# Second layer in the order of the code with follow-ups one block late, expert tokens fetched earlier, and a third float64 piece converted beside the experts

## The chip, the cores and the metric

The kernel runs on one core of a Trainium2 chip. The metric is the device time of one execution in microseconds. It was measured in three runs, and their median counts. A fourth execution was profiled, and its trace is what the rows below come from. Engines are named as in the profile: PE is the matrix engine and PEld its weight load, DVE the vector engine, ACT the scalar engine, POOL the GpSimd engine, and SP issues most transfers.

## What is computed

Attention on 2 x 8 heads of 576 tokens gives 1152 tokens of 512 numbers. A top-1 mixture of eight experts follows, then a second layer for all tokens, the part that most of the change concerns:

```python
h = np.maximum(np.einsum('ecd,edf->ecf', disp, w1), 0.0)   # 8 experts, 512 -> 1024
y = np.einsum('ecf,efd->ecd', h, w2)                        # 1024 -> 512
out[i] = gate_w[i] * y[expert_idx[i], pos[i]]               # kept tokens, others 0
...
h = x @ w_in                                                # 512 -> 2048
g = h * (1.0 / (1.0 + np.exp(-h)))
return (g @ w_out).astype(np.float32)                       # 2048 -> 512
```

The weights `w_in` and `w_out` arrive as float64. The kernel turns them into float32 with integer operations on their words.

## The kernel before

**Experts.** The sixteen units of `WSEQ` alternate: unit 0 is `w1` of expert 0, then `w1` of expert e and `w2` of expert e-1 in turn, so unit 5 is `w1` of expert 3. A `w1` unit multiplies the 192 tokens of its expert, which a transposing transfer (`load_x`, L712) puts into one of two tiles `xw`. Its weights are split into a high and a low float16 part: ACT squares them (L145), a matmul with ones sums over partitions (L150), ACT and DVE write the high halves (L189, L191), DVE the low halves (L196). A `w2` unit works in float32 (L782). Its result goes from `psy` to `yg` (`post_y`, L791, DVE), and ACT squares it (L798). `post_y` needs the gates: `gl` is written to memory and read back into `yg` (L698, L899). Between two units stands `rest()`, a test whether an expert has more than 192 tokens (L918). It has loops inside that don't run here.

**Conversion.** Eight pieces (`in` 0 to 3 and `out` 0 to 3) of 2 MB are each loaded (`c_load`, L843), converted in four parts of three DVE operations (`c_conv`, L850 to L852), squared on ACT (`c_sq`, L858), scaled (`c_scale`) and split, high on POOL (L881) and low on DVE (L882). These steps stand in a list `extra`, of which `task` and `more` take one after the other. Two staging tiles hold a piece: `stg` and `stg2`, the second in a tile of the experts' weights.

**Second layer.** `l1(j, n, fo)` is a block of 12 matmuls of 384 columns into one of four `psh` tiles. Behind it come a sigmoid on ACT (L1113), a product on DVE (L1115), a float16 copy on ACT (L1116) and a remainder on POOL (L1117). `l2(h, i, tt)` is a block of 24 matmuls of 256 columns into one of three `psy` tiles, with a copy on ACT (h = 0, L1135) or a sum on DVE (h = 1, L1137), and at the end a transfer of 128 rows to the output. Order: 24 blocks of `l1`, 18 of `l2`, 24, 18. `split_y` makes the two float16 parts of `yg` that `l1` reads: high (L1071 on ACT, L1073 on POOL) and low (L1074 on DVE).

**Order.** Each engine works through its own queue in order. Under `tc.manual_schedule` that queue is in the order of the code. Elsewhere the compiler's scheduler sets it. Before, units 0 to 3 and from unit 4 to `split_y` are in code order; the blocks of the second layer are the scheduler's.

Of the kernel before, what the change touches and what calls it, by code (L numbers as in the profile page):

```python
# [21 lines left out]
E = 8  # L22
# [14 lines left out]
def moe_kernel(tc, qL, qtL, kL, vL, sL, wgL, w1L, w2L, capL, winL, woutL, out):  # L37
# [680 lines left out]
    def moe_phases():  # L718
# [104 lines left out]
        seq = [("in", 0), ("in", 1), ("out", 0), ("out", 1), ("in", 2), ("in", 3), ("out", 2), ("out", 3)]  # L823
# [37 lines left out]
        def c_scale(m, j):  # L861
            ps = psy.tile([P, 512], F32, tag="y", name="psy")
# [8 lines left out]
        def c_split(m, j, q):  # L871
# [5 lines left out]
            else:  # L877
# [3 lines left out]
            G.tensor_scalar(hi, src, d["s"][q], 0.0, op0=ALU.mult, op1=ALU.add)  # L881
            V.scalar_tensor_tensor(out=lo, in0=src, scalar=d["s"][q], in1=hi,  # L882
                                   op0=ALU.mult, op1=ALU.subtract)
            if q == 3:
                d["done"] = True

        def c_tasks(m, j):
            t = [[] for _ in range(5)]
# [3 lines left out]
            t.append([lambda: c_scale(m, j)])  # L892
            for q in range(4):
                t.append([lambda q=q: c_split(m, j, q)])
# [89 lines left out]
        def unit0():  # L984
            load_x(1)
            slots0()
# [15 lines left out]
        def unit(u):  # L1002
# [5 lines left out]
            if kind == "w1":  # L1008
# [3 lines left out]
                if e < E - 1:  # L1012
                    load_x(e + 1)
# [3 lines left out]
            for q in range(4):  # L1017
# [26 lines left out]
        extra += [[lambda: c_load("in", 0)], []] + c_tasks("in", 0)  # L1044
        extra += [[lambda: c_load("in", 1)], []] + c_tasks("in", 1)
        extra[-1] += [lambda: c_load("out", 0), lambda: c_load("out", 1)]
        for u in range(4, NW):
            unit(u)
        flush(0)
        task(len(extra))  # L1050
        return xctx, cd, c_load, c_tasks, seq, ys, wint, psh, psy, yp, inv
# [3 lines left out]
    def moe2(xctx, cd, c_load, c_tasks, seq, ys, wint, psh, psy, yp, inv):  # L1055
# [5 lines left out]
        yh = y2p.tile([P, 2, 4, NTOK], F16, tag="yh", name="yh")  # L1061
        V.tensor_reduce(out=yt, in_=ysq, axis=AX.X, op=ALU.add)
        ps = pools["psn"].tile([P, 512], F32, tag="n", name="psn")
# [3 lines left out]
        def split_y(n):  # L1067
            a = slice(n * CH, (n + 1) * CH)
            for k in range(4):
                if n == 0:  # L1070
                    A.activation(out=yh[:, 0, k, a], in_=ys[:, k, a], func=AF.Copy, scale=sy)  # L1071
                else:
                    G.tensor_scalar(yh[:, 0, k, a], ys[:, k, a], sy, 0.0, op0=ALU.mult, op1=ALU.add)  # L1073
                V.scalar_tensor_tensor(out=yh[:, 1, k, a], in0=ys[:, k, a], scalar=sy, in1=yh[:, 0, k, a],  # L1074
                                       op0=ALU.mult, op1=ALU.subtract)

        split_y(0)
        k3, k4, rg = inv[:, 0:4], inv[:, 8:12], inv[:, 24:26]
        extra = []
# [3 lines left out]
        for i in range(2, 8):  # L1083
            extra += c_tasks(*seq[i])
            if i + 2 < 8:
                extra[-1].append(lambda i=i: c_load(*seq[i + 2]))
# [12 lines left out]

        def l1(j, n, fo):  # L1100
# [11 lines left out]
            sg = g2p.tile([P, CH], F32, tag="sg", name="sg")  # L1112
            A.activation(out=sg, in_=ps[:, 0:CH], func=AF.Sigmoid, scale=k3[:, j:j + 1])  # L1113
            r = g2p.tile([P, CH], F32, tag="r2", name="r2")
            V.scalar_tensor_tensor(out=r, in0=ps[:, 0:CH], scalar=C1, in1=sg, op0=ALU.mult, op1=ALU.mult)  # L1115
            A.copy(gt[n][:, 0, f, :], r)  # L1116
            G.tensor_tensor(out=gt[n][:, 1, f, :], in0=r, in1=gt[n][:, 0, f, :], op=ALU.subtract)  # L1117

        def l2(h, i, tt):
# [10 lines left out]
            if tt == 0:  # L1130
                if i == 0:
                    V.tensor_scalar(rg[:, h:h + 1], ry, inv[:, 16 + h:17 + h], 1.0 / C1, op0=ALU.mult, op1=ALU.mult)
                V.tensor_tensor(out=kc, in0=rg[:, h:h + 1], in1=cd["out", 2 * h + i]["r"], op=ALU.mult)
            if h == 0:
                A.activation(out=ot[:, tt, d], in_=o, func=AF.Copy, scale=kc)  # L1135
            else:
                V.scalar_tensor_tensor(out=ot[:, tt, d], in0=o, scalar=kc, in1=ot[:, tt, d],  # L1137
                                       op0=ALU.mult, op1=ALU.add)
            if h == 1 and i == 1:
                G.indirect_dma_start(out=out, out_offset=bass.IndirectOffsetOnAxis(ap=idl[:, tt:tt + 1], axis=0),  # L1140
                                     in_=ot[:, tt, :], in_offset=None)

        split_y(1)
        split_y(2)
        man2.close()
        ot = yp.tile([P, NT, DM], F32, tag="yg", name="ot")
# [278 lines left out]
```

## Time and profile before

| | us |
|---|---|
| median of 3 runs | 528.86 |
| lowest and highest | 525.57, 533.93 |
| profiled execution, its own time | 533.83 |
| its span, first to last instruction | 532.2 |

The profiled execution is 4.97 us slower than the median, and 1.63 us of its time lie outside the span. PE is busy in 86% of the span (459.8 us), but it is not busy evenly, so the views of single stretches say more than this share. Times in the rows are us from the start of the span.

### The profile page before, as it was taken

The page shows a single profiled execution, that of the slowest core. Times are in us where ns is not written, and L with a number is a line of the kernel's source. Part 1 is how long each engine was busy: PE and PEld are TensorE (multiplying, and loading weights), DVE is VectorE, ACT ScalarE, POOL GpSimd, SP SyncE. Part 2 cuts the span into 40 slices and gives each one's busy share as a digit, 9 for nine tenths or more (in the row PEclk, how much of TensorE's full clock was granted, in tenths as well). Part 3 has the DMA queues.
Part 4 walks back from the last instruction along what each step waited for, and adds up shares of the span by engine and source line. Part 5 has one row for each costly group of instructions (what it writes and reads, how often), then busy time and mean ns, then how long its engine had stood idle before and what let it go on. Part 6 is the DMA issues. An engine that isn't in the chain of part 4 may idle for free.

```text
span 532.2 us, 9871 instructions
## 1 busy us (share of the span) xinstructions
PE 459.8 (86%) x3788; PEld 375.4 (71%) x3789; DVE 321.7 (60%) x823; ACT 224.9 (42%) x443; POOL 206.3 (39%) x238
## 2 busy tenths in 40 slices
PE   0868579697899994999999987598999999999995
PEld 0744445386689993999999983364688876668885
DVE  8888669996665232954754369999337836321111
ACT  1666537585164305743642026355621534551000
POOL 9775577655136100003000207484541237542121
PEclk9977879999899997899999997899999999999999
DMA  8799999999938849996962171422004400000111
GB/s 153 236 180 219 194 216 217 254 239 201 257 120 276 240 162 292 405 352 205 309 212 91 69 275 43 156 60 101 2 2 160 159 1 0 1 1 20 60 52 49
DMA packets 97122, 83.05 MB, mean 156 GB/s; under 512 B 70112, under 2 KB 74400, under 8 KB 96816
## 3 DMA queue, kind: packets, MB, share of 16 engines
q1 hardware_dynamic: 94112, 76.02, 53.7%
q0 software_dynamic: 1728, 4.76, 2.7%
q10 hardware_dynamic: 1232, 1.61, 1.2%
q8 instruction: 31, 0.51, 0.4%
q14 instruction: 19, 0.16, 0.1%
HBM read 58.07 MB, written 7.91 MB: 124 GB/s over the span
## 4 chain that ended last, share of the span: by engine, by line
PE 42%; DVE 10%; DMA 10%; issue 3%; POOL 1%; ACT 1%; SPq 0%; POOLq 0%; DVEq 0%; ACTq 0%
PE psy L1127 13%; PE psh L1108 11%; PE psy L782 10%; PE psh L753 8%; DMA stg<-in_moe_w_out_dram 3%; DMA xw<-table 2%; DVE cx L851 2%; DMA gl<-gk 2%; DVE yh L1074 2%; DVE cx L850 1%; DVE stg L852 1%; DVE r L1115 1%; DMA meta<-table,srow 1%; DMA wst<-in_moe_w_dram 1%; DVE wout L882 1%
## 5 line engine op out<-in xcount | busy, mean ns | idle before, releaser
L1108 PE MATMUL psh<-yh,win 128*128 128x384 f16 x576 | 99.4, 335 | 9.8 <-DVE r L1115 8.0
L1127 PE MATMUL psy<-wout,g 128*128 128x256 f16 x864 | 95.6, 273 | 1.2 <-ACT ot L1135 1.2
L1108 PEld LDWEIGHTS <-win 128*128 128x128 f16 x576 | 57.6, 100 | 50.0 <-issue 9.5
L1127 PEld LDWEIGHTS <-g 128*128 128x128 f16 x864 | 84.6, 98 | 11.5 <-issue 1.4
L340 PE MATMUL pss<-kt,qa 65*128 65x128 f32 (+3 forms) x128 | 52.8, 560 | 21.7 <-DVE wsp L303 12.0
L1117 POOL TENSOR_TENSOR g<-r,g 128x384 f16<-128x384 f32 x48 | 49.0, 1026 | 49.5 <-ACT g L1116 37.0
L881 POOL TENSOR_SCALAR win<-stg,sci 128x512 f16<-128x512 f32 x16 | 16.0, 1015 | 134.3 <-DVE sci L102 134.3
L753 PE MATMUL psh<-xw,wsp 128*128 128x192 f16 x672 | 60.2, 252 | 8.8 <-DMA xw<-table 8.8
L753 PEld LDWEIGHTS <-wsp 128*128 128x128 f16 x672 | 58.0, 101 | 10.1 <-issue 8.1
L1115 DVE SCALAR_TENSOR_TENSOR r<-psh,sg 128x384 f32<-128x384 f32 x48 | 26.5, 553 | 39.8 <-ACT sg L1113 39.7
L340 PEld LDWEIGHTS pss<-kt,qa 128*128 128x128 f32 (+1 forms) x128 | 26.8, 257 | 31.8 <-DVE nm L363 16.5
L381 ACT ACTIVATE et<-et,nm 128x128 f32<-128x128 f32 (+3 forms) x64 | 32.8, 554 | 28.1 <-DVE nm L363 28.1
L782 PE MATMUL psy<-h,wsp 128*128 128x192 f32 x256 | 42.6, 327 | 0.4 <-PEq L918 0.4
L405 POOL TENSOR_TENSOR hl<-et,hl 128x512 f16<-128x512 f32 (+3 forms) x34 | 35.9, 1066 | 16.9 <-ACT hl L400 15.1
L782 PE MATMUL psy<-h,wst 128*128 128x192 f32 x256 | 42.4, 327 | 0.0
L782 PEld LDWEIGHTS psy<-h,wsp 128*128 128x128 f32 x256 | 41.5, 190 | 0.7 <-PEq L918 0.7
L782 PEld LDWEIGHTS psy<-h,wst 128*128 128x128 f32 x256 | 41.5, 190 | 0.0
L758 ACT ACTIVATE h<-psh 128x384 f32<-128x384 f32 x32 | 15.6, 487 | 57.4 <-PE psh L753 53.3
L1116 ACT CAST g<-r 128x384 f16<-128x384 f32 x48 | 24.4, 508 | 28.1 <-DVE r L1115 28.1
L363 DVE CUSTOM_DVE_ANT_0 et<-pss,mk 128x128 f32<-128x128 f32 (+3 forms) x64 | 28.9, 479 | 9.8 <-POOL hl L405 9.5
L196 DVE SCALAR_TENSOR_TENSOR wsp<-wst,sci,wsp 128x2048 f16<-128x2048 f32 x12 | 28.1, 2339 | 9.1 <-ACT wsp L189 8.3
L1137 DVE SCALAR_TENSOR_TENSOR ot<-psy,inv,ot 128x256 f32<-128x256 f32 x18 | 8.7, 484 | 37.6 <-PE psy L1127 37.6
(248 smaller groups left out, 809.6 us busy)
## 6 DMA issues: line engine op xcount, KB each, us to landing
wst<-in_moe_w_dram SPq DMA_DIRECT2D x42, 512.0 KB, 6.0
wsp<-in_moe_w_dram SPq DMA_DIRECT2D x20, 512.0 KB, 7.7
stg<-in_moe_w_in_dram SPq DMA_DIRECT2D x16, 512.0 KB, 5.4
stg<-in_moe_w_out_dram SPq DMA_DIRECT2D x16, 512.0 KB, 5.5
table<-xh SPq DMA_DIRECT2D x4, 774.0 KB, 6.8
wst<-in_v_dram SPq DMA_DIRECT2D x2, 1024.0 KB, 5.7
kt<-in_k_dram SPq DMA_DIRECT2D x3, 512.0 KB, 7.9
qa<-in_q_dram SPq DMA_DIRECT2D x3, 512.0 KB, 6.1
```

Of the source, the lines that this page charges most:

```text
L196: V.scalar_tensor_tensor(out=d["sp"][:, 1, lo:hi], in0=d["st"][:, lo:hi], scalar=d["s"], in1=d["sp"][:, 0, lo:hi], op0=ALU.mult, op1=ALU.s ...
L340: PE.matmul(out=pv[:, j, :], lhsT=qa[c % 2][r, h, b, :], rhs=kt[r, h, b, 0:n], start=True, stop=True)
L363: maxi[i] = V.tensor_tensor_reduce(out=ev[:, j, :], in0=st[i]["s"][:, j, :], in1=mk[:, 512 - n:512], scale=-0.125, scalar=3.0e38, op0=ALU. ...
L381: A.activation(out=e[:, j, :], in_=e[:, j, :], func=AF.Exp, scale=-1.0, bias=st[i]["m"][j])
L405: spl[i] = (V if LO[i] == "V" else G).tensor_tensor(out=hl[:, w:w + n], in0=e, in1=hl[:, 0:n], op=ALU.subtract)
L753: PE.matmul(out=pv[:, j, :], lhsT=sp[:, cw, k, a], rhs=xw[e][:, 4 * cx + k, :], start=(n == 0 and k == 0), stop=(n == 2 and k == 3))
L782: PE.matmul(out=pv[:, j - js[0], :], lhsT=w[:, k, a], rhs=hh[e][:, k, :], start=(k == 0), stop=(k == 7))
L1108: PE.matmul(out=ps[:, 0:CH], lhsT=wv[:, cw, k, fo * P:(fo + 1) * P], rhs=yh[:, cy, k, a], start=(i == 0 and k == 0), stop=(i == 2 and k == 3))
L1115: V.scalar_tensor_tensor(out=r, in0=ps[:, 0:CH], scalar=C1, in1=sg, op0=ALU.mult, op1=ALU.mult)
L1116: A.copy(gt[n][:, 0, f, :], r)
L1117: G.tensor_tensor(out=gt[n][:, 1, f, :], in0=r, in1=gt[n][:, 0, f, :], op=ALU.subtract)
L1127: PE.matmul(out=o, lhsT=gt[n][:, cg, k, a], rhs=woutt[h][:, cw, k, d], start=(m == 0 and k == 0), stop=(m == 2 and k == 7))
```

## The change

It has four parts. The tokens of experts 1 and 2 are both fetched in unit 0, and those of expert e + 3 at the start of the `w2` unit of expert e; `rest()` moves from behind unit 3 to behind unit 4. The steps of a conversion are spread over twelve places of the list in place of ten, `in` 2 goes through the experts' stage in place of a part of `out` 0, and later pieces follow in another order. The second layer is put under `manual_schedule`, and what follows a block is issued behind the matmuls of the next block (`after1`) or of the next but one (`after2`). The parts of `yg` are made by ACT and DVE without POOL, the first 384 tokens ahead and the others two steps behind each of the first eight blocks.

```diff
@@ load order, conversion
-                if seq.index((m, j)) % 2 and len(cd) > 1:
+                if (m, j) in (("out", 0), ("in", 3), ("out", 3)):
...
-            ps = psy.tile([P, 512], F32, tag="y", name="psy")
+            ps = pools["psn"].tile([P, 512], F32, tag="n", name="psn")
...
+            t = [[] for _ in range(12)]
             for q in range(4):
                 t[q].append(lambda q=q: c_conv(m, j, q))
                 t[q + 1].append(lambda q=q: c_sq(m, j, q))
+                t[6 + q].append(lambda q=q: c_split(m, j, q, 0))
+                t[7 + q].append(lambda q=q: c_split(m, j, q, 1))
+            t[6].insert(0, lambda: c_scale(m, j))
+            if nxt:
+                t[11].append(lambda: c_load(*nxt))
@@ experts
         def unit0():
             load_x(1)
+            load_x(2)
...
-                if e < E - 1:
-                    load_x(e + 1)
+            elif k + 2 < E:
+                load_x(k + 2)
...
-                if u >= 4 and (q == 3 or q and kind == "w2"):
+                if u >= 5 and (q in (0, 3) or kind == "w2"):
...
-        for u in range(1, 4):
+        for u in range(1, 5):
...
+        c_load("in", 0)
+        extra += [[], []] + c_tasks("in", 0, ("in", 1)) + [[]] + c_tasks("in", 1, ("in", 2)) + [[]]
+        extra += c_tasks("in", 2, ("out", 1))
+        for u in range(5, NW):
+            if u == 13:
+                c_load("out", 0)
             unit(u)
         flush(0)
-        task(len(extra))
@@ second layer
+        extra += c_tasks("out", 0, ("in", 3)) + c_tasks("out", 1, ("out", 2)) + c_tasks("in", 3, ("out", 3))
+        extra += c_tasks("out", 2) + c_tasks("out", 3)
...
+        def behind():
+            todo = after2 + after1
+            del after1[:], after2[:]
+            for f in todo:
+                f()
...
+            behind()
+            after1.append(post)
...
-        split_y(1)
-        split_y(2)
-        man2.close()
...
                         l1(2 * h + j, n, fo)
-                        more(1 if h == 0 and j == 1 else fo % 2)
+                        if ysplits:
+                            for _ in range(2):
+                                ysplits.pop(0)()
+                        elif h == 0 or fo % 2:
+                            more()
...
+        behind()
+        man2.close()
```

On SP, in units 0 to 4, `xw<-table` is a fetch of tokens, `wst` and `wsp` are weights of the experts, `gl` and `yg<-gl` the gates. Before:

```order
L131 DMA wst<-in_moe_w_dram 128x1024 x3
L712 DMA_TRANSPOSE xw<-table 128x8x192
L131 DMA wst<-in_moe_w_dram 128x2x512 x3
L131 DMA wst<-in_moe_w_dram 128x1024 x4
L131 DMA wsp<-in_moe_w_dram 128x2x512 x4
L712 DMA_TRANSPOSE xw<-table 128x8x192
L698 DMA gl<-gk 128x9x1
L899 DMA yg<-gl 128x1152
L131 DMA wst<-in_moe_w_dram 128x1024 x4
L131 DMA wst<-in_moe_w_dram 128x2x512 x4
L712 DMA_TRANSPOSE xw<-table 128x8x192
```

After, at the same place:

```order
L131 DMA wst<-in_moe_w_dram 128x1024 x3
L712 DMA_TRANSPOSE xw<-table 128x8x192 x2
L131 DMA wst<-in_moe_w_dram 128x2x512 x3
L131 DMA wst<-in_moe_w_dram 128x1024 x4
L131 DMA wsp<-in_moe_w_dram 128x2x512 x4
L712 DMA_TRANSPOSE xw<-table 128x8x192
L698 DMA gl<-gk 128x9x1
L902 DMA yg<-gl 128x1152
L131 DMA wst<-in_moe_w_dram 128x1024 x4
L131 DMA wst<-in_moe_w_dram 128x2x512 x4
L712 DMA_TRANSPOSE xw<-table 128x8x192
```

The tokens of expert 3 were the last of these rows, behind the gates and two sets of weights; now they stand ahead of `gl`, and the last row fetches those of expert 4.

On DVE, at the end of the experts, L791 is `post_y`, `cx` and `stg` a conversion, `yt` the sum with which the second layer begins. Before:

```order
L791 SCALAR_TENSOR_TENSOR yg<-psy,KY,yg 128x192
L850 TENSOR_SCALAR cx<-stg 128x512
L851 SCALAR_TENSOR_TENSOR cx<-stg,cx 128x512
L852 SCALAR_TENSOR_TENSOR stg<-stg,cx 128x512
L791 ISA
L791 SCALAR_TENSOR_TENSOR yg<-psy,KY,yg 128x192
L850 TENSOR_SCALAR cx<-stg 128x512
L851 SCALAR_TENSOR_TENSOR cx<-stg,cx 128x512
L852 SCALAR_TENSOR_TENSOR stg<-stg,cx 128x512
L850 TENSOR_SCALAR cx<-stg_3676 128x512
L1062 TENSOR_REDUCE yt<-ysq 128x1
```

After, at the same place:

```order
L791 SCALAR_TENSOR_TENSOR yg<-psy,KY,yg 128x192
L791 ISA
L791 SCALAR_TENSOR_TENSOR yg<-psy,KY,yg 128x192
L1068 TENSOR_REDUCE yt<-ysq 128x1
L100 TENSOR_SCALAR sci<-psn 128x1
L101 TENSOR_SCALAR sci<-sci 128x1
L102 TENSOR_SCALAR sci<-sci 128x1
L1075 TENSOR_SCALAR yh<-yg,sci 128x384 x2
```

The conversions between the last two `post_y` and ahead of `yt` are gone from there.

On DVE, at the first blocks of `l1`, `yh` is a low part of `yg`, `wout` a low part of `out` 0, and L1115 (L1132 after) the product behind a block. Before:

```order
L1074 SCALAR_TENSOR_TENSOR yh<-yg,sci,yh 128x384 x8
L851 SCALAR_TENSOR_TENSOR cx<-stg_3676,cx 128x512
L1074 SCALAR_TENSOR_TENSOR yh<-yg,sci,yh 128x384
L882 SCALAR_TENSOR_TENSOR wout<-stg,sc,wout 128x2x256 x4
L852 SCALAR_TENSOR_TENSOR stg_3676<-stg_3676,cx 128x512
L1115 SCALAR_TENSOR_TENSOR r_3775<-psh,sg 128x384
L1115 SCALAR_TENSOR_TENSOR r_3794<-psh,sg 128x384
```

After, at the same place:

```order
L1081 SCALAR_TENSOR_TENSOR yh<-yg,sci,yh 128x384 x4
L1126 TENSOR_TENSOR inv<-sci 128x1
L1132 SCALAR_TENSOR_TENSOR r_3792<-psh,sg 128x384
L1132 SCALAR_TENSOR_TENSOR r_3813<-psh,sg 128x384
L1081 SCALAR_TENSOR_TENSOR yh<-yg,sci,yh 128x384 x2
L1132 SCALAR_TENSOR_TENSOR r_3834<-psh,sg 128x384
L1081 SCALAR_TENSOR_TENSOR yh<-yg,sci,yh 128x384 x2
```

The first product stood behind twelve low parts of `yg`, four of `out` 0 and a conversion; it now stands behind four low parts, and the others come between products.

## Rows read from the trace of the kernel before

**Rows 1.** Timeline, first matmuls of unit 2: start, length, instruction.

```profile
173.16 1.01 PE L782 MATMUL psy<-h,wst 128*128 128x192 f32 x5
```

**Rows 2.** Chain that ended last, experts: start us, length us, what.

```profile
215.08 6.73 PE psh L753 x72
...
232.24 1.98 PE psh L753 x24
...
234.36 5.96 PE psh L753 x72
```

**Rows 3.** Timeline of units 3 to 5: start, length, instruction, [idle before it <-releaser].

```profile
196.60 1.14 DVE L791 SCALAR_TENSOR_TENSOR yg<-psy,KY,yg 128x384 f32 x2 [6.44 <-DMA yg<-gl]
...
197.51 5.44 PE L782 MATMUL psy<-h,wsp 128*128 128x192 f32 x32 [0.45 <-PEq L918]
...
204.63 2.35 DVE L196 SCALAR_TENSOR_TENSOR wsp<-wst,sci,wsp 128x2048 f16<-128x2048 f32 x1 [6.77 <-ACT wsp L189]
204.88 1.90 ACT L145 ACTIVATE junk<-wst 128x2048 f16<-128x2048 f32 x1
...
210.81 4.00 PE L753 MATMUL psh<-xw,wsp 128*128 128x192 f16 x24 [7.86 <-DMA xw<-table]
```

**Rows 4.** Timeline of SP's queue, 160 to 245 us: start and length of issuing.

```profile
161.38 1.42 SPq L712 DMA_TRANSPOSE xw<-table  x1
...
171.89 7.61 SPq L712 DMA_TRANSPOSE xw<-table  x1
181.03 0.37 SPq L698 DMA_DIRECT2D gl<-gk  x1
...
197.98 7.58 SPq L712 DMA_TRANSPOSE xw<-table  x1
```

**Rows 5.** Transfers, 158 to 176 us, rate in 40 slices of 0.45 us.

```profile
GB/s 0 0 0 92 394 101 0 0 0 0 46 200 288 304 337 273 291 207 101 351 369 382 282 391 414 403 414 394 420 404 437 391 386 401 419 405 374 401 423 382
```

**Rows 6.** Timeline from the last expert to the second layer.

```profile
317.61 0.41 DVE L791 SCALAR_TENSOR_TENSOR yg<-psy,KY,yg 128x192 f32 x1
...
320.75 0.17 DVE L1062 TENSOR_REDUCE yt<-ysq 128x1 f32<-128x18 f32 x1 [0.48 <-ACT junk L798]
...
321.43 0.15 DVE L100 TENSOR_SCALAR sci<-psn 128x1 int32<-128x1 int32 x1
...
323.04 2.12 ACT L1071 ACTIVATE yh<-yg,sci 128x384 f16<-128x384 f32 x4
```

**Rows 7.** Timeline of PE in the second layer.

```profile
311.78 5.20 PE L782 MATMUL psy<-h,wsp 128*128 128x192 f32 x31
...
323.70 10.65 PE L1108 MATMUL psh<-yh,win 128*128 128x384 f16 x48 [1.81 <-ACT yh L1071]
339.67 7.57 PE L1108 MATMUL psh<-yh,win 128*128 128x384 f16 x36 [5.33 <-DVE r L1115]
...
361.04 6.01 PE L1108 MATMUL psh<-yh,win 128*128 128x384 f16 x36 [1.20 <-DVE r L1115]
367.76 2.11 PE L1108 MATMUL psh<-yh,win 128*128 128x384 f16 x12 [0.71 <-DVE r L1115]
370.62 13.81 PE L1108 MATMUL psh<-yh,win 128*128 128x384 f16 x84 [0.74 <-DVE r L1115]
...
422.09 10.64 PE L1127 MATMUL psy<-wout,g 128*128 128x256 f16 x96 [1.17 <-ACT ot L1135]
...
440.34 39.16 PE L1108 MATMUL psh<-yh,win 128*128 128x384 f16 x240
```

**Rows 8.** One stretch: length, busy PE, PEld, DVE, ACT, POOL, granted clock, DMA share, GB/s.

```profile
339.70:370.60 30.90, 28.26 (x165) 16.58 (x166) 30.62 (x48) 17.54 (x42) 20.58 (x17) 0.95 0.39 136
```

**Rows 9.** Groups on DVE, 340 to 372 us: busy us, mean ns of one.

```profile
L852 DVE SCALAR_TENSOR_TENSOR stg<-stg,cx 128x512 int32<-128x512 int32 x8 | 9.8, 1226 | 0.2
```

**Rows 10.** Groups on DVE, 395 to 430 us.

```profile
L852 DVE SCALAR_TENSOR_TENSOR stg<-stg,cx 128x512 int32<-128x512 int32 x8 | 5.5, 693 | 0.2
L850 DVE TENSOR_SCALAR cx<-stg 128x512 int32<-128x512 int32 x8 | 3.4, 428 | 4.8 <-DMA stg<-in_moe_w_out_dram 4.7
```

More of the change, by code (lines that the diff above doesn't have):

```diff
@@ L880, in c_split, with c_tasks @@
                 src = src.rearrange("p (k d) -> p k d", d=2 * P)
[L881 to L888, printed above, removed]
+            if part == 0:
+                G.tensor_scalar(hi, src, d["s"][q], 0.0, op0=ALU.mult, op1=ALU.add)
+            else:
+                V.scalar_tensor_tensor(out=lo, in0=src, scalar=d["s"][q], in1=hi,
+                                       op0=ALU.mult, op1=ALU.subtract)
+                if q == 3:
+                    d["done"] = True
+        def c_tasks(m, j, nxt=None):
+            t = [[] for _ in range(12)]
             for q in range(4):
@@ L891, in c_tasks @@
                 t[q + 1].append(lambda q=q: c_sq(m, j, q))
-            t.append([lambda: c_scale(m, j)])
-            for q in range(4):
-                t.append([lambda q=q: c_split(m, j, q)])
+                t[6 + q].append(lambda q=q: c_split(m, j, q, 0))
[3 more added lines that the diff above has]
+                t[11].append(lambda: c_load(*nxt))
             return t
@@ L1043, in moe_phases, with moe2 @@
         man2.enter_context(tc.manual_schedule(engines=ME))
[L1044 to L1047, printed above, removed]
+        c_load("in", 0)
[4 more added lines that the diff above has]
+                c_load("out", 0)
             unit(u)
         flush(0)
-        task(len(extra))
-        return xctx, cd, c_load, c_tasks, seq, ys, wint, psh, psy, yp, inv
+        return xctx, cd, c_load, c_tasks, extra, ys, wint, psh, psy, yp, inv
     woutt = []
-    def moe2(xctx, cd, c_load, c_tasks, seq, ys, wint, psh, psy, yp, inv):
+    def moe2(xctx, cd, c_load, c_tasks, extra, ys, wint, psh, psy, yp, inv):
         mctx = pools["ctx"]
@@ L1111, in l1, with post, post2 @@
                 V.tensor_tensor(out=k3[:, j:j + 1], in0=ry, in1=cd["in", j]["r"], op=ALU.mult)
[L1112 to L1117, printed above, removed]
+            def post():
+                sg = g2p.tile([P, CH], F32, tag="sg", name="sg")
+                A.activation(out=sg, in_=ps[:, 0:CH], func=AF.Sigmoid, scale=k3[:, j:j + 1])
+                r = g2p.tile([P, CH], F32, tag="r2", name="r2")
+                V.scalar_tensor_tensor(out=r, in0=ps[:, 0:CH], scalar=C1, in1=sg, op0=ALU.mult, op1=ALU.mult)
+                def post2():
+                    A.copy(gt[n][:, 0, f, :], r)
+                    G.tensor_tensor(out=gt[n][:, 1, f, :], in0=r, in1=gt[n][:, 0, f, :], op=ALU.subtract)
+                after2.append(post2)
+            behind()
+            after1.append(post)
         def l2(h, i, tt):
@@ L1129, in l2, with post @@
             kc = k4[:, 2 * h + i:2 * h + i + 1]
[L1130 to L1141, printed above, removed]
-        split_y(1)
-        split_y(2)
-        man2.close()
-        ot = yp.tile([P, NT, DM], F32, tag="yg", name="ot")
+            def post():
+                if tt == 0:
+                    if i == 0:
+                        V.tensor_scalar(rg[:, h:h + 1], ry, inv[:, 16 + h:17 + h], 1.0 / C1,
+                                        op0=ALU.mult, op1=ALU.mult)
+                    V.tensor_tensor(out=kc, in0=rg[:, h:h + 1], in1=cd["out", 2 * h + i]["r"], op=ALU.mult)
+                if h == 0:
+                    A.activation(out=ot[:, tt, d], in_=o, func=AF.Copy, scale=kc)
+                else:
+                    V.scalar_tensor_tensor(out=ot[:, tt, d], in0=o, scalar=kc, in1=ot[:, tt, d],
+                                           op0=ALU.mult, op1=ALU.add)
+                if h == 1 and i == 1:
+                    G.indirect_dma_start(out=out, out_offset=bass.IndirectOffsetOnAxis(ap=idl[:, tt:tt + 1], axis=0),
+                                         in_=ot[:, tt, :], in_offset=None)
+            behind()
+            after1.append(post)
+        ysplits = [lambda n=n, k=k, f=f: f(n, k) for n in (1, 2) for f in (split_y, split_y2) for k in range(4)]
         for h in range(2):
@@ L1152, in moe2 @@
                         l1(2 * h + j, n, fo)
-                        more(1 if h == 0 and j == 1 else fo % 2)
+                        if ysplits:
[3 more added lines that the diff above has]
+                            more()
+            if h == 0:
+                ot = yp.tile([P, NT, DM], F32, tag="yg", name="ot")
             need("out", 2 * h)
@@ L1160, in moe2 @@
                 more(2)
+        behind()
+        man2.close()
     zt = []
```

33 lines of the change are left out of this document (16 added, 17 removed).

## The prediction

> **What bounds the kernel now.** I read the busy share by slices first, then the chain of waits, then the timeline of PE wherever the chain leaves PE. PE sets the time nearly everywhere from the experts on, and it stands still or runs slowly in five places. The first is unit 5: PE sits idle for 7.86 us until `xw`, the tokens of expert 3, has landed [rows 3], and then runs its first 24 matmuls in 4.00 us and the next 72 in 6.73 us [rows 2, 3], where the same unit one expert later takes 1.98 and 5.96 us [rows 2]. The second is the join between experts and second layer: the last matmul of the experts ends at 316.98 (311.78 + 5.20) and the first of the second layer begins at 323.70 [rows 7]. The third is a wait of 5.33 us after the first four blocks, for a product on DVE [rows 7]. The fourth is three more waits of that kind, 1.20, 0.71 and 0.74 us, and one of 1.17 us for a copy on ACT [rows 7]. The fifth is the clock, 0.95 of full speed as granted in the stretch that follows the third [rows 8], and lower in the first 48 matmuls: they take 10.65 us, where 240 later ones take 39.16, which is 0.163 each and 7.8 for 48 [rows 7]. In that stretch DVE is busy for 30.62 of 30.90 us [rows 8]: it, and not PE, sets the pace there.
>
> **The tokens fetched earlier.** SP works in order. Expert 3's fetch is issued at 197.98, because ahead of it stand the writing of the gates (181.03), their reading back, and two sets of weights [rows 4]. After the change it stands ahead of the gates and waits only for unit 1 to free its tile, which is at the start of unit 2, 173.16 [rows 1]. It then lands some 20 us before PE needs it. What goes: 7.86 us of idle PE, and the slow restart, 4.00 - 1.98 + 6.73 - 5.96 = 2.79 us, together 10.65 us. What is late next at 202.95, where unit 4 ends (197.51 + 5.44 [rows 3])? The test of `rest()` now stands there; it cost PE 0.45 us in the middle of unit 4 [rows 3], and I charge 0.45. The low halves of unit 5's own weights: DVE does them behind the two `post_y` that wait for the gates, 196.60 + 1.14 + 2 x 2.35 = 202.4 [rows 3], in time. Before, they came at 204.63, because ACT wrote the high half behind a square that waited for a load; the new order puts the high half ahead. The squares of unit 7's weights, whose sum PE takes behind the first 24 matmuls of unit 5: PE now asks at 202.95 + 0.45 + 1.98 = 205.4, and the second square ended at 206.8 before [rows 3], with the moved high half ahead of it; so 0 to 1.4 us, of which I take 0.7. Net: 10.65 - 0.45 - 0.7 = 9.5 us. With a wait this short the restart at low clock has no reason.
>
> **What that fetch is moved past.** The fetch of expert 2's tokens, too, goes forward, ahead of three loads of unit 2's weights. Expert 1's fetch (128 x 8 x 192 numbers of 2 bytes, 0.39 MB) and those loads (1.57 MB) are through at about 169.5, summed from the rates [rows 5]; unit 2 begins at 173.16 [rows 1], which leaves 3.6 us. A fetch that runs alone moves at 200 to 340 GB/s (slices 12 to 17 of [rows 5]), so the second one delays the loads by some 2 us: free. If SP needs 7.61 us to issue it, as behind eleven loads, and not the 1.42 us of the first [rows 4], the loads start at 170.4 and PE waits up to 3 us. I take nothing, since the queue ahead of it is as empty as ahead of the first, and keep 3 for the range. The gates' own write stood at 181.03; the fetch ahead of it may hold it up by 1.7 us (its issue, 7.6 us, begun at about 175), and behind it wait the reading back, `post_y` of expert 0 and with it the second half of unit 4. That is in the same 3 us.
>
> [...]
>
> **The third piece in the experts' stage.** `in` 2 brings four conversions there, and the same number of `out` 0 leaves the last unit: no DVE time is added. From unit 6 on PE is bound by its own matmuls, with the weights' arithmetic hidden. The conversions that remain between matmuls are now under the hand order, two places before the scale, so that PE doesn't wait for a square. I cost this at nothing; the cover is that a conversion is three operations of 0.43 to 0.69 us without POOL beside it [rows 10], against 18.4 us of PE per pair of units (1.98 + 5.96 and about twice 5.2 [rows 2, 7]).
>
> **The join.** Before, DVE had conversions that waited for a load between the last `post_y` and `yt`. After, the chain is `post_y` (0.41 from about 317.1 [rows 6]), a square on ACT (about 0.5, by the wait of `yt` for it), then from `yt` at 320.75 to PE at 323.70 what it is now, 2.95 us [rows 6, 7], less one conversion operation of 0.69 [rows 10] that stood between: 0.1 + 0.41 + 0.5 + 2.26 = 3.3 us in place of 6.72. Saved 3.4. The slow first 48 matmuls (10.65 - 7.8 = 2.8) I keep as they are; if the shorter pause keeps the clock up, up to 2.8 more is saved.
>
> **The first blocks.** The fifth block waits for the first product to free a `psh` tile. That product stood behind twelve low parts of `yg`, four of `out` 0 and a conversion; now it stands behind four low parts. The 5.33 us go, and with them the lowered clock of the stretch behind, 0.05 x 30.9 = 1.5 us [rows 8]. The waits of 1.20 + 0.71 + 0.74 + 1.17 = 3.8 us go with the conversions that move from the first blocks into the loop of `l2`.
>
> **What the hand order adds.** In the first 24 blocks four conversions of `out` 0 remain. With one conversion per block DVE needs 2.86 us per block (367.76 to 370.62 [rows 7]) where PE needs 39.16 / 20 = 1.96 [rows 7]: 0.9 late per block, 3.6 after four. Four `psh` tiles let the product be some 4 us late before PE waits (three blocks, 5.9 us, less the sigmoid and the product themselves), so it just fits; 0 to 2 us. In the 18 blocks of `l2`, about 2.66 us each (10.64 / 4 [rows 7]), the copies on ACT stand behind squares that wait for conversions, with three `psy` tiles: there are twelve conversions of 1.8 us (L851 taken as L852, [rows 10]) for 47 us of PE, and the longest run is four in about 8 us, in which PE has two spare tiles; 0 to 3 us. I take 1.5 for both, since DVE's conversions are short there, without POOL's remainders (0.69 against 1.23 for L852 [rows 9, 10]). Putting follow-ups behind the next block's matmuls costs nothing on PE, since its own queue holds only matmuls.
>
> **The sum.** 9.5 + 3.4 + 5.3 + 1.5 + 3.8 - 1.5 = 22.0 us. Against the profiled execution's own time that gives 533.83 - 22.0 = 511.8. That execution is 4.97 over the median. If its excess lies in the waits that go, the median loses only 17 and also ends at 511.8; if not, it ends at 528.86 - 22.0 = 506.9. I take 509.
>
> **The rivals.** First, the next late load takes the place of `xw`. The weights of units 7 to 9 are issued behind the gates as before, while PE comes 10 us earlier. For it: transfers run at 390 to 440 GB/s [rows 5], the most the trace shows. Against: one pair of units needs 4 MB, 11 us of transfer in 18.4 of PE. Only the second layer gains: 12.5, or 516.4. Second, the hand order gives back in the second layer what it saves, since one late operation at the head of DVE's or ACT's queue now holds up all behind it, where the scheduler had filled in. For it: such a wait was what held `post_y` up at the join. Against: the new order has each load several blocks ahead of its conversion. Then only the 9.5 of the experts stay: 519.4. Third, slower: every later fetch now stands on SP ahead of the next unit's weights and waits for PE to free its tile. If these weights have no slack, each of five fetches costs PE the 7.58 us of its issue [rows 4]: 528.86 - 22.0 + 37.9 = 544.8. It decides from the point where weights land after their unit begins; against it, a fetch is released at the end of a `w1` unit, and the tile for the next weights falls free only about a `w2` unit later. That PE's clock stays up at the join and nothing new waits is a better case: 22.0 + 2.8 + 1.5 + 1.1 = 27.4, 501.5.
>
> **How the numbers follow.** Forecast (504 to 514) 0.63, the better case 0.08, first rival 0.14, second 0.11, third 0.03, no change 0.01. A measurement here can tell about 2% from no change, which is 518.3. Faster by over 2%: 0.63 + 0.08 + 0.14 = 0.85; within 2%: 0.12; slower: 0.03. The range from 501 to 519 takes in the better case, the first rival and half of the second, and leaves out less than 2 in 10 beyond these, with the unknown costs of 3 + 3 + 2 us above the forecast inside it.
>
> **What would show it.** In the new profile PE should start unit 5 less than 2 us after unit 4 and run it in about 8 us; the pause at the join should be 3 to 4 us; the list of waits should have no PE wait over 2 us for a product; the second layer, from the end of the experts to PE's last matmul, should be 12 to 13 us shorter than before. I am wrong if PE waits for weights in units 6 to 9, or if L1132 or L1162 show up as releasers of PE for more than 5 us in sum.

## The result, and the profile after

The changed kernel takes 524.92 us (median of 12 runs, 519.70 to 529.18), the kernel before, run beside it, 530.42 (12 runs). The ratio is 0.9894, with a 95% interval from 0.9853 to 0.9935: 1.1% faster, clear of no change and short of the 2% that counts as a gain here. I had forecast 509, and the range ended at 519. Ratios leave out executions that some disturbance made slower, so they need not be the quotients of the medians. The profiled execution took 527.22 us, 6.6 less than that of before.

First PE's timeline, units 1 to 5 of the changed kernel (start, duration, engine, line, operation, tiles, shape, count; in brackets the idle time ahead and what ended it):

```profile
162.59 2.15 PE L753 MATMUL psh<-xw,wsp 128*128 128x192 f16 x24
...
164.75 1.89 PE L753 MATMUL psh<-xw,wsp 128*128 128x192 f16 x21
166.97 0.24 PE L753 MATMUL psh<-xw,wsp 128*128 128x192 f16 x1 [0.33 <-issue]
...
171.26 0.48 PE L753 MATMUL psh<-xw,wsp 128*128 128x192 f16 x2 [1.70 <-issue]
...
173.40 4.96 PE L753 MATMUL psh<-xw,wsp 128*128 128x192 f16 x40 [0.37 <-issue]
178.20 10.59 PE L782 MATMUL psy<-h,wst 128*128 128x192 f32 x64
...
196.72 10.59 PE L782 MATMUL psy<-h,wsp 128*128 128x192 f32 x64
212.53 4.00 PE L753 MATMUL psh<-xw,wsp 128*128 128x192 f16 x24 [5.22 <-PEq L921]
...
216.66 6.48 PE L753 MATMUL psh<-xw,wsp 128*128 128x192 f16 x72
```

The last 72 matmuls of units 1 and 5 in the kernel before:

```profile
167.22 6.10 PE L753 MATMUL psh<-xw,wsp 128*128 128x192 f16 x72
...
214.94 6.87 PE L753 MATMUL psh<-xw,wsp 128*128 128x192 f16 x72
```

And unit 5 of the changed kernel as a stretch (length, busy PE, PEld, DVE, ACT, POOL, granted clock, DMA share, GB/s):

```profile
212.50:223.00 10.50, 10.47 (x99) 10.27 (x99) 5.34 (x7) 3.36 (x4) 0.00 (x0) 0.76 0.80 280
```

The wait for `xw` before unit 5 [rows 3] is gone, and another stands in its place: 5.22 us behind PE's own queue, at the test of `rest()` (now L921). The unit restarts about as slowly as before, 4.00 and 6.48 us against 4.00 and 6.87 [rows 3], at a granted clock of 0.76 of full speed. In unit 1 there are seven short pauses that no wait explains ("issue"): it takes 15.6 us where it took 8.1. It began 2.5 us earlier than before, so unit 2 starts 5.0 us later, at 178.20 and not at 173.16 [rows 1].

The lines of that test for two engines (count, then shortest, median and longest in ns, then first and last start), in the changed kernel:

```profile
L921 PEldq COMPARE_BRANCH  x1: 7232/7232/7232, 204.8 to 204.8; - x1
L921 DVEq COMPARE_BRANCH  x1: 72/72/72, 207.8 to 207.8; - x1
```

and PE's in the kernel before, where the test stood half a unit earlier:

```profile
L918 PEldq COMPARE_BRANCH  x1: 445/445/445, 194.6 to 194.6; - x1
```

The jump past the path for large experts takes PE's queue 7.23 us in place of 0.45; the other engines need 45 to 72 ns. For the first 2.5 us of it matmuls issued before still run (204.8 to 207.31, the end of unit 4), so 5.22 us are left as a wait. Then the join and the second layer of the changed kernel:

```profile
312.79 5.53 PE L782 MATMUL psy<-h,wsp 128*128 128x192 f32 x33
321.36 0.38 PE L1069 MATMUL psn<-yt,ones 128*128 128x1 f32 x2 [3.05 <-DVE yt L1068]
322.69 19.54 PE L1123 MATMUL psh<-yh,win 128*128 128x384 f16 x108 [0.94 <-DVE yh L1075]
...
342.20 23.56 PE L1123 MATMUL psh<-yh,win 128*128 128x384 f16 x144
...
372.51 0.38 PE L1151 MATMUL psy<-wout,g 128*128 128x256 f16 x2 [0.29 <-POOL wout L880]
374.52 0.58 PE L1151 MATMUL psy<-wout,g 128*128 128x256 f16 x2 [1.63 <-POOL wout L880]
376.53 12.31 PE L1151 MATMUL psy<-wout,g 128*128 128x256 f16 x90 [1.42 <-POOL wout L880]
```

The join is 322.69 - 318.32 = 4.37 us (6.72 before [rows 7]). No block waits for a product any more. At the first of the second products PE waits three times for POOL, which writes the high halves of `out` 0 (3.3 us), and then runs 90 matmuls in 12.31 us, at a granted clock of 0.63 from 376.5 to 383; later, at a granted 1.00, 144 take 15.88, or 9.9 for 90. POOL itself begins late, since it waits for a factor from DVE:

```profile
369.73 0.72 POOL L880 TENSOR_SCALAR wout<-stg,sc 128x512 f16<-128x512 f32 x1 [0.96 <-DVE sc L866]
```

PE's last matmuls, in the changed kernel and in that of before:

```profile
514.74 5.29 PE L1151 MATMUL psy<-wout,g 128*128 128x256 f16 x47
...
514.82 11.84 PE L1127 MATMUL psy<-wout,g 128*128 128x256 f16 x107
```

By stretches, after against before: the start of unit 2 is 5.0 us later; from there to unit 5 3.3 less; the rest of the experts 0.4 less; the join 2.35 less; from the first to the last matmul of the second layer (322.69 to 520.03, against 323.70 to 526.66) 5.6 less. Together 6.6 less, the difference of the profiles.

### The profile page after: what moved, and what is told of

Its sections match the earlier page's. It is cut to its first block, busy times and chain, and to the rows that moved or that the text cites. A ratio compares the mean times of both kernels' runs of the same rounds, so it can differ in the third digit from the quotient of the medians.

```text
span 525.5 us, 9880 instructions
## 1 busy us (share of the span) xinstructions
PE 461.9 (88%) x3788; PEld 376.2 (72%) x3789; DVE 324.7 (62%) x825; ACT 230.1 (44%) x449; POOL 192.4 (37%) x230
## 5 line engine op out<-in xcount | busy, mean ns | idle before, releaser
L1151 PE MATMUL psy<-wout,g 128*128 128x256 f16 x864 | 98.1, 277 | 3.4 <-POOL wout L880 3.4
L1123 PE MATMUL psh<-yh,win 128*128 128x384 f16 x576 | 96.2, 330 | 0.9 <-DVE yh L1075 0.9
L1151 PEld LDWEIGHTS <-g 128*128 128x128 f16 x864 | 85.7, 99 | 15.1 <-issue 4.0
L340 PE MATMUL pss<-kt,qa 65*128 65x128 f32 (+3 forms) x128 | 54.3, 579 | 20.2 <-DMA kt<-wsp 12.6
L753 PE MATMUL psh<-xw,wsp 128*128 128x192 f16 x672 | 62.7, 255 | 9.9 <-PEq L921 5.2
L880 POOL TENSOR_SCALAR win<-stg,sci 128x512 f16<-128x512 f32 x16 | 14.9, 947 | 123.6 <-DMA xw<-table 76.3
L1132 DVE SCALAR_TENSOR_TENSOR r<-psh,sg 128x384 f32<-128x384 f32 x48 | 26.6, 554 | 32.7 <-ACT sg L1130 32.5
L758 ACT ACTIVATE h<-psh 128x384 f32<-128x384 f32 x32 | 15.6, 488 | 67.1 <-PE psh L753 56.3
L152 DVE TENSOR_REDUCE sc<-psn 128x1 f32<-128x4 f32 (+1 forms) x14 | 2.2, 159 | 53.1 <-PE psn L150 40.5
```

The costliest lines, as they stand in the source:

```text
L340: PE.matmul(out=pv[:, j, :], lhsT=qa[c % 2][r, h, b, :], rhs=kt[r, h, b, 0:n], start=True, stop=True)
L753: PE.matmul(out=pv[:, j, :], lhsT=sp[:, cw, k, a], rhs=xw[e][:, 4 * cx + k, :], start=(n == 0 and k == 0), stop=(n == 2 and k == 3))
L1123: PE.matmul(out=ps[:, 0:CH], lhsT=wv[:, cw, k, fo * P:(fo + 1) * P], rhs=yh[:, cy, k, a], start=(i == 0 and k == 0), stop=(i == 2 and k == 3))
L1151: PE.matmul(out=o, lhsT=gt[n][:, cg, k, a], rhs=woutt[h][:, cw, k, d], start=(m == 0 and k == 0), stop=(m == 2 and k == 7))
```

## The experiments

Times are medians, ratios are to the kernel before, run beside them on the same chip.

**The pauses of unit 1, first try.** One line goes back:

```diff
 def unit0():
     load_x(1)
-    load_x(2)
...
         w_load(wi(("w2", k)))
+        if k == 1:
+            load_x(2)
```

> The changed kernel, but expert 2's tokens are fetched where they were before: on SP behind the loads of unit 1, not right behind expert 1's tokens. All else stays changed. Theory 1: the seven pauses of PE in unit 1 that no wait explains (4.7 us, and the half clock behind them, 15.6 us for a unit that otherwise takes 8) come from this second fetch running beside the first one and the weights. Then unit 1 takes about 8 us again and the time falls by 7 us, from 524.9 to 518. Rival: these pauses have nothing to do with the fetch (an accident of that execution or of where PE's instructions lie): they stay, or the time stays at 525 without them.

527.51 us, 0.9937 (0.9878 to 0.9997), and the pauses stay: unit 1 runs from 160.02 to 174.61. So this Theory 1 falls.

**The test behind unit 3,** in two runs (the second for a closer interval):

```diff
-for u in range(1, 5):
+for u in range(1, 4):
     unit(u)
 man.close()
 flush(0)
 rest()
 man2.enter_context(tc.manual_schedule(engines=ME))
+unit(4)
```

> The changed kernel, but the test for experts over 192 tokens stands behind unit 3 again, not behind unit 4. All else stays changed. Theory 1: PE's conditional jump took 7.23 us there, against 0.45 us in the kernel before, because its target was not at hand and had to be fetched through busy DMA queues; behind unit 3 it takes under 1 us again, unit 5 follows unit 4 without a pause and at full clock, and the time falls by 5.2 + 2.5 = 7.7 us to 517. Rival: PE waits at the test for the other engines, which reach it at 207 to 208 us: then the wait moves with it and the time stays at 523 to 525.

> The changed kernel with the test behind unit 3, a second time, in more rounds, beside the next two. All theories: 523.5, 1.7% below the kernel before; PE's jump 0.4 to 0.7 us.

523.47 us, 0.9831 (0.9777 to 0.9884), and 520.32 us, 0.9716 (0.9648 to 0.9785). On PE the test comes in the middle of unit 4 again, as in the kernel before. PE's line and its timeline in the first:

```profile
L921 PEldq COMPARE_BRANCH  x1: 445/445/445, 203.3 to 203.3; - x1
```

```profile
206.04 5.11 PE L782 MATMUL psy<-h,wsp 128*128 128x192 f32 x30 [0.30 <-PEq L921]
210.99 2.14 PE L753 MATMUL psh<-xw,wsp 128*128 128x192 f16 x24
...
213.14 6.10 PE L753 MATMUL psh<-xw,wsp 128*128 128x192 f16 x72
```

The jump costs 0.45 us again, nothing stands before unit 5, and the unit runs its 24 and 72 matmuls in 2.14 and 6.10 us, the lengths that unit 3 of the changed kernel has at a granted clock of 1.00 (188.6 to 196.7): the wait and the slow restart came with the test's new place. By the ratios the time falls by about 3 us in the first run and 9 in the second, around the 7.7 expected, but only the second's interval lies below that of the changed kernel (0.9853 to 0.9935).

**Without the test,** alone, and with the second fetch put back as in the first try:

```diff
 flush(0)
-rest()
 man2.enter_context(tc.manual_schedule(engines=ME))
```

> The changed kernel without the test and its path for experts of more than 192 tokens (left out; no expert here has so many). Theory 1: without the jump, unit 5 starts behind unit 4 at full clock: 5.2 + 2.5 us less, 517. Rival: the next late thing (the squares of the next weights, SP's loads, which waited 4.1 us for PE at the test) takes its place: 522 to 525.

> Both at once: expert 2's tokens fetched where they were before, and the test and its path for experts of more than 192 tokens left out. Theory 1: the two gains are independent and add up, 7 + 7.7: 510, near the forecast. Rival: both pauses hide the same late work, so that one of them is kept by something else: 517 or more.

The first: 522.09 us, 0.9809 (0.9761 to 0.9856); the second: 524.61 us, with no ratio. Unit 5 starts behind unit 4 without a pause in both, but they are poor tests: with the test gone, SP's queue holds the load of `in` 0 ahead of the tokens. SP in the first, and PE's wait for them:

```profile
155.03 2.18 SPq L841 DMA_DIRECT2D stg<-in_moe_w_in_dram  x4
165.71 3.04 SPq L712 DMA_TRANSPOSE xw<-table  x2
```

```profile
170.32 4.02 PE L753 MATMUL psh<-xw,wsp 128*128 128x192 f16 x24 [4.36 <-DMA xw<-table]
```

So the test had also held a load back: in the changed kernel this one is issued at 212.26.

**The kernel before, a second look.**

> The kernel before, unchanged, for a second profiled execution. All five profiles that start with the changed kernel's front show PE standing still in pieces in unit 1 (unit 1 takes 12 to 16 us), also the one whose fetch of expert 2's tokens is back at its old place; the one profile of before does not (8.1 us). Theory 2: the pauses are not of the change, they come and go between executions of any of these kernels; then this execution may show them, 3 to 8 us. Rival: they belong to the changed kernel, and unit 1 takes 8 us here again.

536.8 us, one execution. PE in unit 1 and at unit 5:

```profile
168.99 0.32 PE L753 MATMUL psh<-xw,wsp 128*128 128x192 f16 x2 [0.24 <-issue]
...
171.99 6.00 PE L753 MATMUL psh<-xw,wsp 128*128 128x192 f16 x36 [1.23 <-issue]
...
213.02 4.00 PE L753 MATMUL psh<-xw,wsp 128*128 128x192 f16 x24 [5.37 <-DMA xw<-table]
```

The pauses are there too: they are not of the change. And the wait for `xw` is 5.37 us where it was 7.86 [rows 3]: with unit 2 begun 4.6 us later, PE begins unit 5 only 2.2 us later, so a late start eats into the wait.

**One part at a time.** The second layer alone (with the third piece, and with fetches and test back at their old places), and the fetches alone on the kernel before, twice; the edit of the latter:

```diff
 def unit0():
     load_x(1)
+    load_x(2)
...
-        if e < E - 1:
-            load_x(e + 1)
+    elif k + 2 < E:
+        load_x(k + 2)
```

> The changed kernel with the fetches of tokens and the test for large experts back at their old places; the second layer in hand order and the third piece converted in the experts' stage stay. Theory: the second layer from the end of the experts on keeps the 8.0 us that the profiles of before and after show (209.7 against 201.7), and the wait for expert 3's tokens before unit 5, 7.9 us, is back: 530.4 - 8.0 = 522.4. Rival (the forecast's size): 12.5 us, 518.

> The kernel before with the fetches of tokens alone moved as in the change; test, experts' stage and second layer as before. Theory of the forecast: unit 5 starts right behind unit 4 at full clock, 10.65 us less: 520. Rival 1: the second fetch delays the loads behind it, unit 1 or unit 2 gives 5 to 8 us back: 525 to 528. Rival 2: PE's start of unit 5 is held by another late load, 527 or more.

> The kernel before with the fetches of tokens alone moved, a second time, on the chip of these runs. Theory 7: the 7.9 us that PE waits for expert 3's tokens in the kernel before are partly a place where a late front is caught up, so that with pauses in unit 1 the earlier fetch gains nothing (532.9 against 533.1), and without them what is left after the wait for the gates in unit 4 (2 to 3 us, and the slow clock behind it): 5 us, 0.990. Rival: the forecast's 9.5 us, 0.982.

The second layer alone: 525.27 us, 0.9863 (0.9748 to 0.9978). The fetches alone: 532.88 us, 0.9989 (0.9921 to 1.0058), in a profile with pauses in unit 1; and 524.39 us, 0.9920 (0.9879 to 0.9962), without them. The gain of the earlier fetch is about 0 and 4 us by these ratios, not 9.5. PE in the second:

```profile
178.58 1.33 PE L753 MATMUL psh<-xw,wsp 128*128 128x192 f16 x14 [1.17 <-DVE wsp L196]
...
191.82 0.56 PE L782 MATMUL psy<-h,wsp 128*128 128x192 f32 x2 [0.58 <-DVE yg L791]
193.24 4.63 PE L782 MATMUL psy<-h,wsp 128*128 128x192 f32 x27 [0.85 <-PEq L918]
...
200.21 2.14 PE L753 MATMUL psh<-xw,wsp 128*128 128x192 f16 x24 [0.93 <-ACT h L758]
```

Unit 5 starts 0.93 us late and at full clock (24 matmuls in 2.14 us), as forecast; but 1.17 us go in unit 3, where DVE is late with the weights' low half, and 0.58 us for the gates.

**The output weights four tasks earlier,** on the kernel with the test behind unit 3:

```diff
 if ysplits:
     for _ in range(2):
         ysplits.pop(0)()
+    if h == 0 and j == 0 and (n, fo) in ((0, 0), (0, 1), (1, 0), (1, 1)):
+        more()
```

> The changed kernel with the test behind unit 3, and with four of the tasks of the hand order begun in the first eight blocks of the second layer (in those blocks in which DVE has no low part of the layer's input to write), so that the first piece of the second layer's output weights is split four blocks earlier. Theory: the three waits of PE for POOL's high halves (3.3 us) and the half clock behind them (2.4 us) go: 5.7 us less than the kernel with the test behind unit 3 (523.5), 518. Rival: DVE, full in those blocks, holds up the products instead, and PE waits as long in the first blocks: 523.

520.77 us, 0.9742 (0.9627 to 0.9856). Its profile has the second layer no shorter (315.51 to 514.0, against 318.98 to 517.3). What PE waits for there (us in all, times, longest):

```profile
PE psn L150 <- ACT stg L856: 4.5, 2, 4.0
PE psn L1070 <- DVE yt L1069: 3.0, 1, 3.0
```

The waits for POOL are gone, and PE waits 4.0 us for ACT's squares of the next piece: the rival had the place wrong, but was right that another wait would come instead.

**What the jump waits for.** First with expert 4's tokens fetched behind the test, then with 128 more instructions of PE ahead, at last with a shorter path to jump over:

```diff
-    elif k + 2 < E:
+    elif k + 2 < E and u != 4:
         load_x(k + 2)
...
 rest()
 man2.enter_context(tc.manual_schedule(engines=ME))
+load_x(4)
```

> The changed kernel with the test left behind unit 4, but expert 4's tokens fetched behind the test and not at the start of unit 4, so that the DMA queues hold less when PE jumps. Theory 3: PE's jump is long because the instructions at its target come through DMA queues that are full of this fetch and the weights (their first packet starts 4.8 us after the jump); then the jump takes 3 us or less in place of 7.2, unit 5 starts under 1.5 us after unit 4, and the time falls by 4 to 7 us from 524.9, to 519. Rival: a jump whose target is not at hand costs 7 us whatever the queues hold: 7.2 us again, and 525.

```diff
+def pad(n):
+    for _ in range(n):
+        PE.matmul(out=win["warm"][:, 0:8], lhsT=ident16, rhs=vhl[:, 0, 0].rearrange("p h b d -> p (h b d)")[:, 0:8],
+                  start=True, stop=True)
...
         warm(4)
+        pad(64)
```

> The changed kernel, test left behind unit 4, with 64 narrow matmuls (128 instructions of PE) added in the routing stage and nothing else: they move where PE's later instructions lie within the blocks of 16 KB in which the trace shows them being fetched. Theory 6: the jump is long only because its target, some 300 instructions on, lies beyond the blocks already there; behind unit 3, 60 instructions earlier, it is still inside. 128 instructions more bring it inside again: the jump takes 0.4 to 0.7 us behind unit 4 too, unit 5 follows at once, and the time falls by 6 us, to 519. Rival: the place behind unit 4 itself (all engines late, queues full) makes it long: 6 to 7.5 us again, 525.

```diff
-for f in range(8):
+for f in range(1):
...
-for d in range(4):
+for d in range(1):
```

> The changed kernel, test left behind unit 4, with the path for experts of more than 192 tokens cut down to one of its eight hidden blocks and one of its four output blocks (the rest of that path is left out; no expert here takes it). PE then jumps over some 90 instructions in place of some 300. Theory 6: the jump is long because its target lies so far on that it isn't among the instructions already fetched; now it takes under 1 us (up to 3.7 us if the next block is still on its way, as with the 64 narrow matmuls), and the time falls by 4 to 7 us, to 515 to 518, or 0.975 to 0.98 of the kernel before. Rival: the place behind unit 4 makes any jump long: 6 to 7.5 us, 0.985 to 0.99.

The last leaves 16 of 68 matmuls (with the transposes) in the path that no expert takes here. In that order: 522.81 us, 0.9811 (0.9741 to 0.9882); 519.97 us, 0.9802 (0.9714 to 0.9890); 522.24 us, 0.9702 (0.9618 to 0.9786). PE's jump in the three:

```profile
L921 PEldq COMPARE_BRANCH  x1: 6132/6132/6132, 203.7 to 203.7; - x1
```

```profile
L921 PEldq COMPARE_BRANCH  x1: 3665/3665/3665, 201.4 to 201.4; - x1
```

```profile
L921 PEldq COMPARE_BRANCH  x1: 353/353/353, 209.5 to 209.5; - x1
```

and PE's timeline in the third:

```profile
201.43 10.59 PE L782 MATMUL psy<-h,wsp 128*128 128x192 f32 x64
212.47 2.14 PE L753 MATMUL psh<-xw,wsp 128*128 128x192 f16 x24 [0.45 <-PEq L921]
```

Over the shorter path the jump at the very same place costs 0.35 us, and unit 5 starts 0.45 us after unit 4 at full clock (2.14 us). So the place alone doesn't make a jump long; and the length of the path alone doesn't either, since the whole path costs 0.45 us behind unit 3. Theory 3 explains 1 us at most (6.1 against 7.2, and 6.45 in another execution of the changed kernel). The queues while PE jumped in the changed kernel, first 204.8 to 209.6, then 209.6 to 210.8 (packets, MB, share):

```profile
q1 hardware_dynamic: 1734, 0.82, 126.5%
...
```

```profile
q8 instruction: 1, 0.02, 5.7%
```

The page lists q8 as a queue of instructions, with 31 packets and 0.51 MB, so blocks of some 16 KB. It moves nothing for 4.8 us, then one block, which begins at 209.65 and takes 1.09 us; 1.3 us after that PE is through. In the second execution of the changed kernel, whose jump begins at 199.4 and takes 6.45 us, q8 brings one block between 199 and 206; with 128 instructions more, in a jump of 3.67 us from 201.4 on, one between 201 and 206; in the kernel before, whose jump takes 0.45 us at 194.6, none between 193.6 and 197.5. So the three long jumps go with a block that comes in during these stretches, and the short one with none. That the block holds the jump's target is my reading: no view shows what is in it. How long the jump is depends here on both, where the test stands and how far it jumps: behind unit 4 it took 6.13 to 7.45 us over the whole path, 3.67 with 128 instructions more ahead and 0.35 over the shorter path; behind unit 3, over the whole path, 0.45. Theory 6 forecast 0.4 to 0.7 us with the 128 instructions; why 3.67 remain, no run shows.

**The front, last tries.** The two edits that put back the second fetch and the test, together; and, with the test behind unit 3, the gathers of the gates moved behind unit 1:

> The same with expert 2's tokens fetched at their old place, behind the weights of unit 1. Theory 4: the early second fetch costs what the profiles show from the start of unit 0 to the start of unit 2 (27.4 us on average in four with it, 23.1 in four without): 4 us less than the kernel with the test behind unit 3, 519.5. Rival: that difference is chance, the pauses of unit 1 come and go in either order: 523.5 as the other.

```diff
-for t in range(NT):
-    slots_g(t)
...
-if u == 2:
+if u == 3:
     slots1()
     load_gates()
...
+if u == 1 and q == 3:
+    G.tensor_scalar(hold, hh[1][:, 4, 0:1], 1.0, 0.0, op0=ALU.mult, op1=ALU.add)
+    for t in range(NT):
+        slots_g(t)
```

> The changed kernel with the test behind unit 3, and with the nine small gathers of gates and slots that POOL issues during units 0 and 1 held back until unit 1 is nearly through. Theory 5: PE's pauses in unit 1 come from these gathers (nine in 10 us) beside the loads: unit 1 takes 8 us without a pause, though the later gates may hold up unit 4. Rival: they come with the loads of weights alone: unit 1 takes 12 to 16 us as before.

521.74 us, 0.9754 (0.9693 to 0.9815), beside 0.9716 with the early fetch: no gain, Theory 4 falls. The gathers: 532.77 us, 0.9968 (0.9924 to 1.0011). None of the four profiles of these runs has pauses in unit 1, so Theory 5 stays untested. The second shows what the gates are worth; its unit 4:

```profile
213.28 3.57 PE L782 MATMUL psy<-h,wsp 128*128 128x192 f32 x12 [13.82 <-DVE yg L791]
```

**The changed kernel again, and all mended.**

> The changed kernel, unchanged, beside these on one chip. All theories: 1% below the kernel before, 0.985 to 0.993 of it; PE's jump 6 to 7.5 us again, the three waits for POOL's high halves 3.4 us again; unit 1 with or without pauses, as the chip has them.

> The changed kernel with all that the runs pointed to: the test behind unit 3; expert 3's tokens fetched behind the writing of the gates; the last squares' queue emptied before the last products of the experts; two tasks of the second layer's hand order begun in its first two blocks, and one task instead of two behind each of the first three blocks of the second product. Theory: against the kernel with the test behind unit 3 alone (523.5 and 520.3) the wait of PE for the gates in unit 4 (2.8 and 1.7 us of half clock), 1.4 us at the join and 4 of the 5.7 us at the output weights go: 512 to 515. Rival: as in the kernel with four tasks begun early, PE waits elsewhere for the same DVE work: 518 to 521.

```diff
-    elif k + 2 < E:
+    elif k + 2 < E and u != 2:
         load_x(k + 2)
     if u == 2:
         slots1()
+        load_x(k + 2)
         load_gates()
...
+while late:
+    late.pop(0)[1]()
 flush(0)
...
+    if h == 0 and j == 0 and n == 0 and fo < 2:
+        more()
...
     l2(h, i, tt)
-    more(2)
+    more(1 if h == 0 and i == 0 and tt < 3 else 2)
```

The changed kernel: 521.61 us, 0.9847 (0.9767 to 0.9928). With no pauses in unit 1, PE meets the gates' wait as well:

```profile
188.65 5.39 PE L782 MATMUL psy<-h,wsp 128*128 128x192 f32 x32
196.41 5.44 PE L782 MATMUL psy<-h,wsp 128*128 128x192 f32 x32 [2.37 <-DVE yg L791]
206.29 4.00 PE L753 MATMUL psh<-xw,wsp 128*128 128x192 f16 x24 [4.44 <-PEq L921]
```

All mended: 508.55 us, 0.9612 (0.9546 to 0.9678), faster than both kernels. What PE still waits for in the experts and the second layer:

```profile
PE psy L782 <- DVE yg L791: 1.8, 1, 1.8
PE psn L1073 <- DVE yt L1072: 1.3, 1, 1.3
PE psy L782 <- issue: 1.2, 1, 1.2
...
PE psy L1155 <- DVE wout L882: 0.4, 1, 0.4
```

The join is 2.6 us, the output weights cost 0.4 us. Of the wait for the gates, 1.8 of 2.4 us stay: the fetch ahead of them on SP was not its main cause. That this kernel ends near the 509 of the forecast bears nothing out: it has edits that the change had not.

## Why the prediction was wrong

Of the 22.0 us forecast the profiles show 6.6: in the experts 9.5 became a loss of 1.3, at the join 3.4 became 2.35, and in the second layer 9.1 (5.3 + 1.5 + 3.8 - 1.5) became 5.6. In the experts, 5.0 us go to a later start of unit 2, and behind that stand the pauses of unit 1, which come and go and are no step of the prediction: that this profile had them and that of before had not is bad luck. Without them the second profile of the changed kernel took 521.27 us, and its runs gain 1.5%, so the misses below stay.

**"The tokens fetched earlier"** failed, 9.5 us forecast. That the wait for `xw` goes, and that a short wait has no slow restart, was right (the fetches alone: 0.93 us, then 24 matmuls in 2.14 us). Wrong was "I charge 0.45" for the test: I took its price at the old place for its price at the new one. It cost 5.22 us and kept the restart slow: unit 5 runs from 212.53 to 223.14, which is 2.4 us more than the same unit with the test behind unit 3 (210.99 to 219.24). The test behind unit 3 and the short path behind unit 4 both give these back in the profile.

**"What that fetch is moved past"** was 0 with 3 in reserve. PE waits 2.37 us for the gates where nothing ahead delays it, and 1.17 us for weights in unit 3 with the fetches alone. Moving the one fetch behind the gates' write took 0.6 us off, so it is chiefly that PE comes to them earlier: in the second profile of the changed kernel it is through the first half of unit 4 at 194.04 in place of 197.06, and goes on behind the gates at 196.41, where before DVE had them at 196.60 [rows 3]. And the 7.86 us were a cushion: in a profile with pauses in unit 1 the kernel before loses only 5.37 us there, and the fetches alone gained nothing in the runs whose profile had pauses. That the pauses made this difference rests on one profile of each kind. The one profile of before, without pauses, could not show it.

**The third piece** was right: from unit 5 on the experts take 105.8 us, against 106.2.

**"The join"** was right in kind, 2.35 us in place of 3.4. I counted one square on ACT behind the last product; four stand there, from 318.87 to 321.11. Emptying that queue first brought PE's wait for `yt` from 3.05 to 1.26.

**"The first blocks"** was right: all waits for products are gone.

**"What the hand order adds"** was mis-sized: 1.5 forecast, and measured 3.3 for three waits on POOL and 12.31 - 9.9 = 2.4 at a lower clock behind them. I weighed products and copies and left out the high halves of `out` 0, which are split with the last four of the 24 blocks, behind its conversions on DVE. With the gains of the first blocks (5.3 + 1.5 + 3.8), 10.6 - 5.7 = 4.9, near the 5.6 seen from the first to the last matmul.

None of the rivals names the jump, and neither sign of being wrong came. Weights were not late in units 6 to 9, so the first and the third did not come; the second had the right mechanism at another place, for part of the gain.

## What to carry to other kernels

The branch here had no price of its own. The same jump took PE 0.45 us behind unit 3 and 7.23 behind unit 4, and over a shorter path 0.35 there, so before one is moved, count the instructions that it skips, and afterwards look at its own line on every engine. The idle stretch of PE before unit 5 was also a cushion for what was late ahead of it, 7.86 us in one profile of the kernel before and 5.37 in another, and one profile did not tell how much of it was free. In an order written by hand, follow every engine that writes an operand up to the first matmul that reads it, POOL too, whose high halves cost 3.3 us of waiting here.

## What I had not expected of the hardware

PE's pauses in unit 1 (1.3 to 8.4 us more for a unit of 8.1) go with groups of runs made together, whatever the kernel. Of the seventeen profiles of the experiments, all eight of two groups on one chip have them, none of the eight of two groups on two other chips, and then a later one on one of these. During them other engines are late too: in the changed kernel ACT reads the first block only at 169.93, though its matmuls ran until 164.7, and the profile shows no wait for that time. What causes the pauses stays open. It is not the place of the second token fetch: they are there with it early, late, and in the kernel before. Whether it is the gathers is untested, since that run came where there were no pauses.
